# Second MoE in two phases per 768 tokens: gated values kept in SBUF, the output by seven block products, weights split once and streamed

## The chip, the cores and the metric

The kernel runs on one core of one Trainium2 chip. The metric is the device time of one execution in microseconds, as the median of several runs. A core has TensorE (matmuls, with a separate record for each weight load), VectorE, ScalarE, GpSimd and SyncE; here SyncE issues the DMAs. In the profile they are PE and PEld, DVE, ACT, POOL, and SP or SPq.

## What is computed

Three layers, one after the other, in float32:

```python
# attention, 4 x 8 heads x 768 positions x 64, chunks of 32 with a window of 56 and 8 memory keys
a = exp(scores - max); a = a / (sum(a) + 1e-09); out[chunk] = a @ v_full
x = out.transpose(0, 2, 1, 3).reshape(3072, 512)
# first MoE, d_ff = 2048
h = x @ w_in;  y = max(h, 0) ** 2 @ w_out
# second MoE, d_ff = 1536
g = y @ w_gate;  silu = g / (1 + exp(-g))
result = (silu * (y @ w_val)) @ w_out2          # 3072 x 512
```

Weights come as 64-bit floats and are turned into float32 on the chip. For precision each float32 operand is split into a high half (rounded to the matmul's type, float32r) and a low half (the rest), and each product is three passes: high x high, high x low, low x high.

## The kernel before

Attention for eight blocks of 384 tokens runs beside the first MoE. The first MoE works by block t and by f (16 blocks of 128 hidden columns): `hidden` (L413) issues 12 matmuls into one of two banks `hbank`, `relu`, `square`, `square_again` and `square_lo` make the halves of the squared values on ScalarE and VectorE, and `project` (L434) issues 12 matmuls into `ybank` two f later. In this part only TensorE's order is written by hand; the other engines' order comes from a planner that goes by its own costs and by due times. A due time is a count of quarter steps of f, `QB` = 64 of them per block.

In blocks 2 to 6 of the first MoE, 18 preps ready the second MoE's weights: `load2` (L455) fetches 1 MB into a tile `raw`, of which there are two, and `prep2` (L458) converts it (ScalarE, VectorE) to a tile `cut`. For two of three preps GpSimd makes four sums of 256 columns, and one to three DMAs store weights and sums, unsplit, to DRAM (`w2g`, `w2o`).

The second MoE takes 768 tokens at a time (s = 0 to 3), as two blocks of 384 tokens, and f = 0 to 11 (128 columns each of gate and value). Gate and value are computed together as a 2x2 block product by the Strassen-Winograd scheme: seven block products instead of eight (`gated`, L571), each of six matmuls of 384 columns, with the token sums T1 to T4 and the weight sums S1 to S4. VectorE combines the results; ScalarE applies Silu. Products alternate between the two banks `hbank`. Weights are loaded again for each f and each s, and split again (ScalarE the high half, GpSimd the low half: `split_w`, L481, through L92 and L95).

The output product follows at once: for each f, 18 matmuls of 512 columns (six groups of 128 tokens, three passes) add into six banks `outs` over all f (`output`, L617). `fill` (L762) puts them between the next f's products, six at a time. At f = 11 the banks are copied out and stored. In the second MoE the order on all engines is written by hand. `split_b1`, `sum_t` and `split_t` (L519 to L542) prepare the next 768 tokens during the current ones.

Of the kernel before, what the change touches and what calls it, by code (L numbers as in the profile page):

```python
# [19 lines left out]
GQ = 96  # L20
# [24 lines left out]
QC = 2 * 128  # L45
RAW = 2048
# [18 lines left out]
def attention_moe_moe_kernel(ctx, tc, att, v0, w1, w2, out):  # L65
# [132 lines left out]
    turned = [yb1[:, i, 0:NI * GQ].rearrange("p (j q) -> p j q", q=GQ) for i in range(2)]  # L198
# [253 lines left out]
    WAT = {n: i * QC for i, n in enumerate(("A11", "A12", "S2", "S3", "S1", "S4", "A22"))}  # L452
    w2t = {}
# [4 lines left out]
    def prep2(c):  # L458
        raw = w.pop(("raw2", c))
        a = convert(raw)  # L460
        if c % 3 == 2:
            sp.dma_start(out=w2o[c // 3], in_=a)
            return
        dst = w2g[c // 3 * 2 + c % 3]
        a11, a12, a21, a22 = (a[:, i * QC:(i + 1) * QC] for i in range(4))
        sums = raw.bitcast(F32)[:, 0:4 * QC]
        s2, s3, s1, s4 = (sums[:, i * QC:(i + 1) * QC] for i in range(4))
        for o, x, y, op in (
            (s1, a21, a22, ALU.add), (s2, s1, a11, ALU.subtract),
            (s3, a11, a21, ALU.subtract), (s4, a12, s2, ALU.subtract),  # L470
        ):
            pool.tensor_tensor(o, x, y, op)  # L472
        sp.dma_start(out=dst[:, 0:2 * QC], in_=a[:, 0:2 * QC])
        sp.dma_start(out=dst[:, 2 * QC:6 * QC], in_=sums)
        sp.dma_start(out=dst[:, 6 * QC:7 * QC], in_=a22)

    def fetch(key, raw, src, n):
        w["raw2", key] = raw[:, 0:n]
        sp.dma_start(out=raw[:, 0:n], in_=src)

    def split_w(key, part):  # L481
        raw = w["raw2", key]
        n = raw.shape[1] // 2
        if part == 0:
            w2t[key] = pair()
        c = slice(n * part, n * part + n)
        split(*(t[:, c] for t in w2t[key]), raw[:, c], act, pool)
# [3 lines left out]

    NGV = (4 * QC, 3 * QC)

    def load_gv(i, half):
        c = 4 * QC * half
        raw = rawp.tile([128, WC], F32, tag="cut", name="gvraw", bufs=CB)
        fetch((i, half), raw, w2g[seq2[i][1], :, c:c + NGV[half]], NGV[half])

    def split_gv(i, half, part):
        split_w((i, half), part)  # L500


    def load_out(i):
        fetch(("out", i), spare(), w2o[seq2[i][1] // 2], WC)

    def split_out(i, part):
        split_w(("out", i), part)
# [10 lines left out]

    def split_b1(s, k):  # L519
        if k == 0:  # L520
            zt[s] = {}
            zt[s]["x"] = [xp.tile([128, KD, NTM], R, tag=f"x{i}", name=f"z{i}") for i in range(2)]
# [4 lines left out]
    def sum_t(s, name):  # L527
# [3 lines left out]
        if name == "T2":  # L531
            t2 = spare()[:, 0:2 * NT2].rearrange("p (k n) -> p k n", k=2)
# [6 lines left out]
    def split_t(s, name):  # L539
        src = zt[s][name]  # L540
        zt[s][name] = [t[:, 0:2 * NT2].rearrange("p (k n) -> p k n", k=2) for t in pair()]
        split(*zt[s][name], src, act, dve)  # L542

    utile = {}

    def product(i, wname, zname, to):
        c = WAT[wname]
        whi, wlo = (t[:, c % WC:c % WC + QC] for t in w2t[i, c // WC])
        zh, zl = zt[seq2[i][0]][zname]
        n = 0  # L550
# [20 lines left out]
    def gated(i, fill, side):  # L571
# [29 lines left out]
        if not late:  # L601
            fill(6)
# [240 lines left out]
```

## Time and profile before

| | |
|---|---|
| median of the runs | 1170.83 us (1170.21 to 1172.29, 3 runs) |
| profiled execution, first to last instruction | 1170.6 us |
| TensorE busy | 1156.5 us, 8156 matmuls |
| VectorE, ScalarE, GpSimd busy | 673.3, 604.0, 354.2 us |
| DMA | 150.78 MB, mean 129 GB/s |

The span covers all work; the runs' median is 0.2 us above it. A listed duration of a matmul includes its way through the array, and matmuls overlap, so the time from one start to the next says what a matmul costs.

### The profile page before, as it was taken

The numbers are of one execution on the slowest core, as the hardware profiler recorded it, in microseconds if no ns is written. First come the engines' busy times: TensorE is split into PE (matmuls) and PEld (weight loads), VectorE is DVE, ScalarE is ACT, GpSimd is POOL, SyncE is SP. The second block draws the span as 40 slices with busy tenths as digits, with TensorE's granted clock in tenths as the row PEclk, the third lists the DMA queues.
The fourth block names the chain that finished last, engine by engine and source line by source line (L and its number), as shares of the span: only waits on it lengthen the run. The fifth ranks groups of instructions, "written<-read, shape, count | busy, mean of one in ns | idle before, by whom it ended". The sixth has DMA issues, their size and how long they took to land.

```text
span 1170.6 us, 20811 instructions
## 1 busy us (share of the span) xinstructions
PE 1156.5 (99%) x8156; PEld 1101.8 (94%) x8156; DVE 673.3 (58%) x1210; ACT 604.0 (52%) x1470; POOL 354.2 (30%) x299
## 2 busy tenths in 40 slices
PE   6999999999999999999999999999999999999998
PEld 5999999999999999999999999999999999999997
DVE  7897435547455474532415576656766576665554
ACT  5897445546455455554543444444445444553432
POOL 0000000203002021000034475555656465654551
PEclk9999999999999999999999999999999999999999
DMA  9732124527144272520124222353234433343231
GB/s 375 291 129 78 55 65 166 181 81 277 58 174 168 77 252 87 169 87 18 56 81 145 99 99 95 136 184 114 89 123 153 149 107 105 100 147 131 84 111 55
DMA packets 49443, 150.78 MB, mean 129 GB/s; under 512 B 4800, under 2 KB 14528, under 8 KB 44992
## 3 DMA queue, kind: packets, MB, share of 16 engines
q1 hardware_dynamic: 49344, 149.44, 36.8%
q8 instruction: 64, 1.05, 0.4%
q14 instruction: 35, 0.29, 0.1%
HBM read 122.68 MB, written 26.74 MB: 128 GB/s over the span
## 4 chain that ended last, share of the span: by engine, by line
PE 98%; DMA 1%; DVE 0%; SPq 0%; ACT 0%; issue 0%; DVEq 0%; ACTq 0%
PE hbank L553 30%; PE hbank L385 23%; PE yb L429 23%; PE yb L627 11%; PE abank L627 6%; PE abank L282 2%; PE abank L160 2%; PE hbank L220 1%; DMA first_v<-in_v_dram 1%; DMA out_dram<-o 0%; PE yb L202 0%; SPq L135 0%; DVE tmp L592 0%; DVE tmp L593 0%; DVE o L631 0%
## 5 line engine op out<-in xcount | busy, mean ns | idle before, releaser
L95 POOL TENSOR_TENSOR w<-gvraw,w 128x512 fp32r<-128x512 f32 x192 | 247.6, 1311 | 294.4 <-ACT w L92 294.4
L385 PE MATMUL hbank<-x,w 128*128 128x384 f32 (+1 forms) x1548 | 293.1, 338 | 0.0
L553 PE MATMUL hbank<-w 128*128 128x384 f32 x1440 | 281.8, 335 | 0.1
L385 PEld LDWEIGHTS hbank<-x,w 128*128 128x128 f32 x1548 | 272.9, 191 | 0.8 <-issue 0.2
L553 PEld LDWEIGHTS hbank<-w 128*128 128x128 f32 x1440 | 254.5, 188 | 9.2 <-DVE tmp L593 0.8
L429 PE MATMUL yb<-gh,w 128*128 128x384 f32 x1024 | 205.0, 337 | 0.0
L429 PEld LDWEIGHTS yb<-gh,w 128*128 128x128 f32 x1024 | 178.7, 188 | 2.2
L410 DVE TENSOR_TENSOR gl<-r,gh 128x384 fp32r<-128x384 f32 x128 | 74.2, 581 | 181.1 <-ACT r L404 180.6
L472 POOL TENSOR_TENSOR wraw<-cut 128x256 f32<-128x256 f32 x24 | 19.7, 842 | 445.7 <-DVE mx L228 285.7
L562 ACT CAST uh<-tmp 128x384 fp32r<-128x384 f32 x96 | 49.4, 514 | 185.1 <-DVE tmp L597 152.4
L393 ACT ACTIVATE r<-hbank 128x384 f32<-128x384 f32 x128 | 63.0, 492 | 146.9 <-PE hbank L385 146.9
L627 PE MATMUL yb<-w,uh 128*128 128x512 f32 x384 | 119.5, 392 | 0.0
L553 PE MATMUL hbank<-z,w 128*128 128x384 f32 x576 | 115.6, 335 | 0.0
L429 PE MATMUL yb<-gl,w 128*128 128x384 f32 x512 | 113.2, 334 | 0.0
L553 PEld LDWEIGHTS hbank<-z,w 128*128 128x128 f32 x576 | 102.1, 188 | 4.2
L92 ACT CAST w<-gvraw 128x512 fp32r<-128x512 f32 x192 | 99.2, 564 | 3.1 <-POOL w L95 2.1
L429 PEld LDWEIGHTS yb<-gl,w 128*128 128x128 f32 x512 | 90.9, 188 | 0.0
L236 ACT ACTIVATE prob<-abank,mx 96x72 f32<-96x72 f32 x224 | 68.2, 317 | 39.4 <-DVE mx L228 39.0
L263 DVE STREAM_TRANSPOSE pT<-prob 32x256 f32<-32x256 f32 x196 | 85.2, 435 | 3.2
L627 PEld LDWEIGHTS yb<-w,uh 128*128 128x128 f32 x384 | 70.7, 188 | 9.2
L627 PE MATMUL abank<-w,uh 128*128 128x512 f32 x192 | 74.9, 397 | 0.0
L399 ACT ACTIVATE gh<-r 128x384 fp32r<-128x384 f32 x128 | 67.4, 528 | 3.3
(97 smaller groups left out, 1278.8 us busy)
## 6 DMA issues: line engine op xcount, KB each, us to landing
wraw<-in_w_dram SPq DMA_DIRECT2D x34, 1024.0 KB, 8.1
gvraw<-w2g SPq DMA_DIRECT2D x48, 512.0 KB, 3.6
gvraw<-w2g SPq DMA_DIRECT2D x48, 384.0 KB, 3.1
qk<-in_att_dram SPq DMA_DIRECT2D x28, 464.0 KB, 3.9
spare<-w2o SPq DMA_DIRECT2D x24, 512.0 KB, 4.4
v<-in_att_dram SPq DMA_DIRECT2D x28, 256.0 KB, 3.5
y1d<-ys SPq DMA_DIRECT2D x8, 768.0 KB, 3.8
w2g<-wraw SPq DMA_DIRECT2D x12, 512.0 KB, 3.1
```

What stands on the lines that cost most here:

```text
L92: act.copy(hi, src)
L95: lo_engine.tensor_tensor(lo, src, hi.bitcast(F32), ALU.subtract)
L236: act.activation(probs[u % 2][:, h, 0:WK], s["s"][:, r, i], AF.Exp, bias=s["mx"][:, r, i:i + 1], scale=SCALE, accum_out=s["sm"][:, h],)
L263: dve.transpose(pT[row:row + 32, :, 32 * c:32 * c + 32], probs[u % 2][32 * c:32 * c + 32, :, col:col + 32],)
L385: pe.matmul(hbank[f % 2][:, cols], wt[:, k * 128:(k + 1) * 128], x[:, k, cols], start=i == 0, stop=i == 3 * KD - 1,)
L393: act.activation(r, hbank[f % 2][:, 0:n], AF.Relu)
L399: act.activation(gh, gtile[t, f]["r"], AF.Square)
L410: dve.tensor_tensor(gl, g["r"], g["gh"].bitcast(F32), ALU.subtract)
L429: pe.matmul(ybank[e][:, 0:nt_of[t]], wt[:, c:c + 128], gtile[t, f][g], start=f == 0 and p == 0, stop=f == NF1 - 1 and p == 2,)
L553: pe.matmul(to, wt[:, k * 128:k * 128 + 128], z[:, k], start=n == 0, stop=n == 5)
L562: act.copy(uh, u)
L627: pe.matmul(outs[j], u[:, c:c + 128], wt, start=f == 0 and p == 0, stop=f == NF2 - 1 and p == 2)
```

## The change

The second MoE keeps its scheme for gate and value, but works in two phases per 768 tokens. In the first phase all 84 gate and value products run one after the other, in four PSUM banks (`abanks`: the two `hbank` and two taken from `yb1`); the gated values u (six pairs of f, each with four blocks A11, A21, A12, A22) stay in SBUF in six tiles `uf`. GpSimd makes the sums S1 to S4 of the blocks of u.

In the second phase the output product is a Strassen-Winograd product too: seven block products (`ITEMS`), each over six pairs p, so 42 items. An item is nine matmuls of 256 columns: three groups of 128 tokens, three passes, with the halves of a block of u as weights and the output weights as moving data. Each block product fills 768 columns of PSUM (`pbank`, two of them in turn), and `combine` adds them up, on VectorE but for the first. The halves of u pass through a ring of ten pairs of tiles; the first ten splits are made in the first phase, each other one ten items ahead of its use. The next tokens are prepared in the second phase.

Weights and weight sums, those of the output weights too, are split in `prep2` and stored as 126 chunks of 256 KB (`w2d`), in the order of use. They are streamed four at a time into five tiles, once per 768 tokens; `load_chunks` for a group is called after the last product of the fifth group ahead of it. The due times of the preps move from (12, 26, 40, 52) to (4, 18, 32, 44) in each block.

The diff, cut to its core:

```diff
+NP = NF2 // 2
+GVC, WOC = 7 * NF2, 7 * NP
+NCH = GVC + WOC
+NRING = 10
...
-    w2g = dp.tile([NF2, 128, 7 * QC], F32, name="w2g")
-    w2o = dp.tile([NF2 // 2, 128, 2 * DM], F32, name="w2o")
+    w2d = dp.tile([128, NCH, 2, QC], F32, name="w2d")
     y1d = dp.tile([128, KD, NTOK], F32, name="y1d")
     hbank = [ps.tile([128, 512], F32, name=f"hbank{i}") for i in range(2)]
-    abank, yb0, yb1 = (ps.tile([128, 2, 512], F32, name=n) for n in ("abank", "yb0", "yb1"))
-    ybank = [b[:, i] for b in (yb0, yb1) for i in range(2)]
+    abank, yb0 = (ps.tile([128, 2, 512], F32, name=n) for n in ("abank", "yb0"))
+    yb1 = [ps.tile([128, 512], F32, name=f"yb1{i}") for i in range(2)]
+    ybank = [yb0[:, 0], yb0[:, 1], *yb1]
...
     def prep2(c):
         raw = w.pop(("raw2", c))
         a = convert(raw)
-        if c % 3 == 2:
-            sp.dma_start(out=w2o[c // 3], in_=a)
+        b0, b1, b2, b3 = (a[:, i * QC:(i + 1) * QC] for i in range(4))
+        sums = raw.bitcast(F32)[:, 0:4 * QC]
+        o0, o1, o2, o3 = (sums[:, i * QC:(i + 1) * QC] for i in range(4))
+        j, kind = divmod(c, 3)
+        if kind < 2:
+            jobs = ((o2, b3, b2, ALU.add), (o0, o2, b0, ALU.subtract), (o1, b0, b3, ALU.subtract), (o3, b1, o0, ALU.subtract))
+            first = 7 * (2 * j + kind)
+            places = [w2d[:, first:first + 3:2], w2d[:, first + 5:first + 6], w2d[:, first + 1:first + 4:2], w2d[:, first + 4:first + 7:2]]
+            parts = ((0, 2), (2, 4))
...
+        for o, x, y, op in jobs:
+            pool.tensor_tensor(o, x, y, op)
+        head = ap.tile([128, 2 * QC], R, tag="head", name="head")
+        pieces = [(a[:, 0:2 * QC], head), (b2, b3.bitcast(R))]
+        act.copy(head, a[:, 0:2 * QC])
+        pool.tensor_tensor(a[:, 0:2 * QC], a[:, 0:2 * QC], head.bitcast(F32), ALU.subtract)
+        act.copy(b3.bitcast(R), b2)
+        pool.tensor_tensor(b2, b2, b3, ALU.subtract)
+        hs = raw.bitcast(R)[:, 4 * QC:8 * QC]
+        act.copy(hs, sums)
+        pool.tensor_tensor(sums, sums, hs.bitcast(F32), ALU.subtract)
+        pieces += [(sums[:, m * QC:n * QC], hs[:, m * QC:n * QC]) for m, n in parts]
+        for place, (lo, hi) in zip(places, pieces):
+            for h, part in enumerate((hi.bitcast(F32), lo)):
+                sp.dma_start(out=place[:, :, h], in_=part.rearrange("p (n c) -> p n c", c=QC))
+
+    chunks = {}
+    NS = NTOK // (2 * NT2)
+
+    def load_chunks(g):
+        if 4 * g >= NS * NCH:
             return
...
+        t = chunks[g] = wp.tile([128, 4, 2, QC], R, tag="w", name="wst")
+        n = 0
+        while n < 4:
+            c = (4 * g + n) % NCH
+            m = min(4 - n, NCH - c)
+            sp.dma_start(out=t[:, n:n + m].bitcast(F32), in_=w2d[:, c:c + m])
+            n += m
...
+    uf, ring = [], []
+    SLOT = {"A11": 0, "A21": 1, "A12": 2, "A22": 3, "S3": 4, "S1": 1, "S2": 0, "S4": 2}
+    ITEMS = ("A11", "A12", "S2", "S3", "A22", "S1", "S4")
+    abanks = [*hbank, *yb1]
+    pbank = [b.rearrange("p a c -> p (a c)")[:, 0:2 * NT2] for b in (abank, yb0)]
...
+    def split_u(s, j, lo_engine):
+        i, p = divmod(j, NP)
+        hi, lo = ring[(WOC * s + j) % NRING]
+        split(hi, lo, u_of(p, ITEMS[i]), act, lo_engine)
...
+        if n % 4 == 3:
+            load_chunks(n // 4 + 5)
+
+    def gated(s, f, side):
+        n0 = NCH * s + 7 * f
+        b0 = 7 * (NF2 * s + f)
+        q = [abanks[(b0 + n) % 4][:, 0:NT2] for n in range(7)]
+        z = zt[s]
+        pair0, pair1, pair2 = double(), double(), double()
+        p1, u2 = pair0[:, 0:NT2], pair0[:, NT2:]
+        g0, u3 = pair1[:, 0:NT2], pair1[:, NT2:]
+        c22, u4 = pair2[:, 0:NT2], pair2[:, NT2:]
...
+    def item(s, j):
+        i, p = divmod(j, NP)
+        uh, ul = ring[(WOC * s + j) % NRING]
+        n = NCH * s + GVC + j
+        whi, wlo = chunk(n)
+        to = pbank[(7 * s + i) % 2]
+        for t in range(3):
+            rows = slice(128 * t, 128 * t + 128)
+            for m, (u, wt) in enumerate(((uh, whi), (ul, whi), (uh, wlo))):
+                pe.matmul(
+                    to[:, QC * t:QC * t + QC], u[:, rows], wt,
+                    start=p == 0 and m == 0 and t != 1, stop=p == NP - 1 and m == 2 and t != 0,
+                )
+        if n % 4 == 3:
+            load_chunks(n // 4 + 5)
...
+    def combine(s, i):
+        p = pbank[(7 * s + i) % 2]
+        if i == 0:
+            acc["x"] = double()
+            act.copy(acc["x"], p)
+        elif i == 2:
+            dve.tensor_tensor(acc["x"], p, acc["x"], ALU.add)
+        elif i == 3:
+            acc["y"] = double()
+            dve.tensor_tensor(acc["y"], p, acc["x"], ALU.add)
+        else:
...
     for c in range(NC2):
-        a = QB * (P2 + c // 4) + (12, 26, 40, 52)[c % 4]
+        a = QB * (P2 + c // 4) + (4, 18, 32, 44)[c % 4]
...
+    for s in range(NS):
+        for p in range(NP):
+            f = 2 * p + 1
+            job((s, f, 0), split_u, s, p, pool)
+            job((s, f, 1), sum_u, p, "S3")
+            last_pair = p == NP - 1
+            key = (s, "b", 0) if last_pair else (s, f + 1, 1)
+            job(key, sum_u, p, "S1")
+            job((s, "b", 0) if last_pair else (s, f + 1, 2), sum_u, p, "S2")
+            if NP + p < NRING:
+                job((s, f + 1, 4), split_u, s, NP + p, pool)
+            job((s, "b", 2 * NP + p), sum_u, p, "S4")
+        for j in range(NRING, WOC):
+            job((s, "b", j - NRING), split_u, s, j, pool if j % 3 == 2 else dve)
+        if s + 1 < NS:
+            job((s, 6, 3), load_z, s + 1)
+            for at_j, fn, *args in (
+                (0, split_b1, 0), (2, split_b1, 1), (4, sum_t, "T1"), (6, sum_t, "T3"), (8, sum_t, "T2"),
+                (10, sum_t, "T4"), (12, split_t, "T2"), (15, split_t, "T3"), (18, split_t, "T1"), (21, split_t, "T4"),
+                (24, split_t, "B22"),
             ):
-                job(i + at_f, slot, fn, s + 1, *args)
-    todo = iter(())
...
+    for s in range(NS):
+        for f in range(NF2):
+            gated(s, f, lambda slot: work(s, f, slot))
+        final = s == NS - 1
+        for j in range(WOC - NP * final):
+            item(s, j)
+            for args in ready:
+                store(*args)
+            ready.clear()
+            if j and j % NP == 0:
+                combine(s, j // NP - 1)
+            work(s, "b", j)
```

For the last 768 tokens the seventh block product runs as three rows of 18 matmuls (`item_rows`), and each row is added and stored by itself.

## Rows read from the trace of the kernel before

**Rows 1.** The page, part 1: busy us (share of the span), instructions, by engine.

```profile
PE 1156.5 (99%) x8156; PEld 1101.8 (94%) x8156; DVE 673.3 (58%) x1210; ACT 604.0 (52%) x1470; POOL 354.2 (30%) x299
```

**Rows 2.** The page, part 4: chain that ended last, by engine.

```profile
PE 98%; DMA 1%; DVE 0%; SPq 0%; ACT 0%; issue 0%; DVEq 0%; ACTq 0%
```

**Rows 3.** That chain in time, second MoE: start us, us, engine, target, line, count.

```profile
1092.01 3.14 PE hbank L553 x18
1095.15 0.47 PE yb L627 x2
...
1096.55 2.08 PE hbank L553 x12
...
1103.50 3.15 PE hbank L553 x18
```

**Rows 4.** Groups by form, second MoE: xcount | busy us, mean ns | idle before <-releaser.

```profile
L627 PE MATMUL yb<-w,uh 128*128 128x512 f32 x384 | 119.5, 392 | 0.0
L627 PE MATMUL abank<-w,ul 128*128 128x512 f32 x96 | 38.1, 397 | 0.0
L553 PEld LDWEIGHTS hbank<-w 128*128 128x128 f32 x1440 | 254.5, 188 | 9.2 <-DVE tmp L593 0.8
```

**Rows 5.** Timelines of TensorE in the opening: start us, us to the last end, what.

```profile
32.17 0.92 PE L385 MATMUL hbank<-x,w 128*128 128x288 f32 x3
32.89 0.49 PE L385 MATMUL hbank<-x,w 128*128 128x96 f32 x2
33.40 2.12 PE L385 MATMUL hbank<-x,w 128*128 128x96 f32 x9
35.32 0.97 PE L385 MATMUL hbank<-x,w 128*128 128x384 f32 x2
```

**Rows 6.** Timeline of weight loads after a stall near the end.

```profile
1159.60 0.30 PEld L553 LDWEIGHTS hbank<-w 128*128 128x128 f32 x2 [0.39 <-DVE tmp L593]
```

**Rows 7.** Groups by form, operations of the other engines that the change repeats or adds.

```profile
L578 DVE TENSOR_TENSOR tmp<-hbank,tmp 128x384 f32<-128x384 f32 x48 | 26.8, 557 | 43.6 <-ACT tmp L575 38.7 <-PE yb L627 3.0 <-PE hbank L553 1.1
L562 ACT CAST uh<-tmp 128x384 fp32r<-128x384 f32 x96 | 49.4, 514 | 185.1 <-DVE tmp L597 152.4 <-DVE tmp L609 31.1 <-PE hbank L553 1.0
L95 POOL TENSOR_TENSOR w<-gvraw,w 128x384 fp32r<-128x384 f32 x96 | 109.1, 1155 | 8.7 <-ACT w L92 8.7
L535 DVE TENSOR_TENSOR zraw<-zraw 128x768 f32<-128x768 f32 x8 | 10.9, 1364 | 3.0 <-DMA zraw<-y1d 3.0
L95 DVE TENSOR_TENSOR w<-zraw,w 128x768 fp32r<-128x768 f32 x16 | 17.7, 1106 | 7.8 <-ACT w L92 7.8
L372 ACT CAST w<-cut 128x1024 fp32r<-128x1024 f32 x16 | 16.8, 1049 | 0.9 <-DVE cut L368 0.9
L472 POOL TENSOR_TENSOR wraw<-cut 128x256 f32<-128x256 f32 x24 | 19.7, 842 | 445.7 <-DVE mx L228 285.7 <-DVE cut L113 119.3 <-DMA v<-in_att_dram 40.7
```

**Rows 8.** Timeline, first MoE, all engines (SPq is SP's DMA queue).

```profile
161.64 0.49 ACT L393 ACTIVATE r<-hbank 128x384 f32<-128x384 f32 x1 [2.46 <-PE hbank L385]
...
167.68 2.25 PE L385 MATMUL hbank<-x,w 128*128 128x384 f32 x12
...
205.21 1.53 POOL L472 TENSOR_TENSOR wraw<-cut 128x256 f32<-128x256 f32 x2 [8.76 <-DVE cut L113]
...
209.67 0.32 SPq L474 DMA_DIRECT2D w2g<-wraw  x1
...
210.51 0.78 SPq L141 DMA_DIRECT2D v<-in_att_dram  x1
```

**Rows 9.** Waits of ScalarE: line, waited for, us in total, times, longest us.

```profile
ACT wraw L110 <- DMA wraw<-in_w_dram: 35.0, 12, 6.2
```

**Rows 10.** Stretch 0 to 30 us: busy by engine, PEclk, DMA share, GB/s.

```profile
0.00:30.00 30.00, 20.21 (x406) 17.94 (x407) 20.86 (x40) 15.58 (x23) 1.75 (x10) 1.00 0.94 376
```

**Rows 11.** Timeline, the last matmul and the copy that follows it.

```profile
1166.01 0.39 PE L627 MATMUL abank<-w,ul 128*128 128x512 f32 x1
1166.76 0.69 DVE L631 COPY o<-abank 128x512 f32<-128x512 f32 x1 [0.94 <-DMA out_dram<-o]
```

More of the change, by code (lines that the diff above doesn't have):

```diff
@@ L489, in spare, with chunk @@
+    def chunk(n):
+        t = chunks[n // 4]
+        return [t[:, n % 4, h] for h in range(2)]
     def spare():
         return wp.tile([128, RAW], F32, tag="w", name="spare")[:, 0:WC]
[L492 to L504, printed above, removed]
@@ new lines, in gated @@
+    def gated(s, f, side):
[7 more added lines that the diff above has]
+        c22, u4 = pair2[:, 0:NT2], pair2[:, NT2:]
+        first, second = (u_of(f // 2, f"A{h}{f % 2 + 1}") for h in (1, 2))
+        product(n0, z["B11"], q[0])
+        act.copy(p1, q[0])
+        side(0)
+        product(n0 + 1, z["T2"], q[1])
+        dve.tensor_tensor(u2, q[1], p1, ALU.add)
@@ L594, in gated @@
         side(5)
-        product(i, "A22", "T4", q)
-        dve.tensor_tensor(u3, u3, q, ALU.subtract)
-        dve.tensor_tensor(u3, u3, g0, ALU.mult)
+        product(n0 + 6, z["B22"], q[6])
+        dve.tensor_tensor(u4, q[6], u4, ALU.add)
+        act.activation(u4, u4, AF.Silu)
+        dve.tensor_tensor(second, c22, u4, ALU.mult)
         side(6)
-        first = halves_of(u3)
-        late = i == len(seq2) - 1
-        if not late:
-            fill(6)
-        product(i, "S4", "B22", p)
@@ new lines, in item_rows, with store @@
+    def item_rows(s, t, to):
+        rows = slice(128 * t, 128 * t + 128)
+        for p in range(NP):
+            j = 6 * NP + p
+            uh, ul = ring[(WOC * s + j) % NRING]
+            whi, wlo = chunk(NCH * s + GVC + j)
+            for m, (u, wt) in enumerate(((uh, whi), (ul, whi), (uh, wlo))):
+                pe.matmul(to, u[:, rows], wt, start=p == 0 and m == 0, stop=p == NP - 1 and m == 2)
+    acc, ready = {}, []
+    def store(s, h, e, o, t0=0, n=3):
+        r0 = (2 * s + h) * NT2 + 128 * t0
+        sp.dma_start(
+            out=out[r0:r0 + 128 * n, e * QC:(e + 1) * QC].rearrange("(t p) c -> p t c", p=128),
+            in_=o.rearrange("p (t c) -> p t c", c=QC),
+        )
@@ L760, in attention_moe_moe_kernel, with job @@
[L760 to L775 removed]
+    def job(key, fn, *args):
+        jobs.setdefault(key, []).append((fn, args))
@@ new lines, in attention_moe_moe_kernel, with work @@
+    for _ in range(2):
+        t = rawp.tile([128, WC], R, tag="cut", name="ring", bufs=CB)
+        ring.append([t[:, 0:NT2], t[:, NT2:2 * NT2]])
+    def work(*key):
+        for fn, args in jobs.pop(key, []):
+            fn(*args)
+    for s in range(NS):
[10 more added lines that the diff above has]
+            work(s, "b", j)
+        if not final:
+            combine(s, 6)
+            for args in ready:
+                store(*args)
+            ready.clear()
```

219 lines of the change are left out of this document (80 added, 139 removed).

## Prediction

> **What bounds the kernel now.** I read the busy shares first: TensorE is busy 99% of the span, VectorE, ScalarE and GpSimd 58, 52 and 30% [rows 1]. A busy TensorE need not be full, so I read next what ended last: 98% of that chain is TensorE, following itself [rows 2]. In order of time the chain shows a steady beat inside the second MoE: 18 products, six output matmuls, 12 products and so on, again at the same place after 1103.50 - 1092.01 = 11.49 us [rows 3]. That is one f (a block of 128 gate and value columns); 48 of them are 551 us, nearly half the span. So the time is set by the columns that TensorE streams: an edit counts if it changes these, or makes TensorE wait where it doesn't now.
>
> The price of a matmul is its step from start to start; listed durations overlap. 18 matmuls of 384 columns take 3.14 us, 0.174 each; six of 512 lie between 1095.15 and 1096.55, 0.233 each [rows 3]: both 2.2 columns per ns, with no fixed part. An f is 42 of the one and 18 of the other; by columns 11.49 us splits into 42 x 0.1741 + 18 x 0.2321 = 7.31 + 4.18.
>
> **The change, part by part.**
>
> *Output product.* Before, 48 x 18 = 864 matmuls of 512 columns (four groups, 384 + 192 + 192 + 96, the first and the last in [rows 4]): 864 x 0.2321 = 200.5 us. After, per 768 tokens seven block products of six k-blocks, 9 matmuls of 256 columns each: 378, in all 1512. No row shows 256 columns with a full 128x128 weight. If columns alone count, a step is 0.1161 us, and all take 175.5 us: a gain of 25.0. The danger is the weight load, as every matmul brings new weights. The [rows 5] show where it bites. The opening ran at TensorE's lower level (1.2 GHz): three steps of 288 columns from 32.17 to 32.89, 0.240 each, 1.2 columns per ns. But nine steps of 96 columns, from 33.40 to 35.32, took 0.213 each and not 0.08. That floor is the load of 128 weight columns, and since 288 columns show nothing of it, a step is the larger of the two, not their sum. At the upper level (2.4 GHz), after a stall, two loads take 0.30 us [rows 6], one of them 0.19 [rows 4], so they start 0.11 apart: the floor halves with the clock. 256 columns at 0.116 stand just above it. I take 0.116, by the row of 288 columns, which is nearest: an eighth above its floor it cost nothing; here the margin is 5%. The ends are 0.11 (166 us, 9 us less) and 0.174 (the step of 384, 263 us, 88 us more).
>
> The Trainium skill (TensorE: Matmul & The Clock Gate, The mechanism) says that weight loads overlap running matmuls only when their row groups differ. All weights here fill the 128 rows, so by it a step would be 0.11 + 0.116 us, and the output products 342 us, 141 more than now. The trace speaks against it: a step of 0.174 leaves no room for 0.11 + 0.174.
>
> *Gate and value products.* The same 2016 matmuls, but with no output matmuls between them, and with four PSUM banks instead of two. Per f VectorE has nine operations of 0.56 (L578) [rows 7], 5.0 us, and one wait for a Silu of some 0.7, against 7.31 us of TensorE; ScalarE has three of about 0.5 and at most one high half of u. A bank is wanted again three products later, 3.1 us; its slowest reader (two adds on one bank) needs 1.1. Cost nothing; if this cover is gone, a gap appears ahead of a product in every f. Gain: the two places where two banks had no filler (TensorE's loads waited for L593, 0.8 us [rows 4], half of it at 1159.60 [rows 6]).
>
> *Splits of u.* In the output phase each item (9 matmuls, 1.04 us) wants one split: ScalarE 0.51, then VectorE 0.56 for two items of three, GpSimd 1.16 for the third [rows 7]. In the first 25 items VectorE also prepares the next tokens: four sums of up to 1.36, seven low halves of 1.11, three block sums that I put at 1.1 for 768 columns, and 17 low halves of u: 5.5 + 7.7 + 3.3 + 9.5 = 26.0 us, in 25 x 1.04 = 26.0 us. It will fall behind a little. Cover: the ring holds ten items (some 8 us of lag), and a block sum's bank is wanted again five items later (about 4 us of lag). I take nothing; with VectorE a quarter slower, a lag of 6.5 us would cost 2 us in each of three phases, 6 us. The weight splits that leave the second MoE were in no chain (GpSimd was 70% idle): no gain.
>
> *Stream of weights.* 126 chunks of 256 KB per 768 tokens, 132 MB in all: 1 MB per 4.17 us, 252 GB/s, with z and outputs about 270. In the first 30 us the queue moved 376 GB/s [rows 10] (the clock column of that row reads 1.00, though the steps of rows 5 just behind it are those of the lower level; I go by the steps). A load is asked for four groups (16.7 us) ahead; SP carries nothing else but two loads of z and the stores, each behind one VectorE sum. Cost nothing; without that cover each late group holds TensorE.
>
> *Preparing in the first MoE.* Eighteen preps now make all sums and all splits. Per prep GpSimd has four sums of 0.84 [rows 7] and three low halves (in proportion to columns 0.8, 1.7 and 3.4), ending some 9 us after the join; ScalarE has three copies (0.4, 0.6, 1.05 by L562 and L372 [rows 7]), 37 us in all; SP has 132 small stores instead of 42. ScalarE's copies wait for GpSimd's sums, and Relu and Square queue behind them. SP's stores wait for GpSimd, and loads of qk and v queue behind those: already before, a load of v left at 210.51 behind a store that had waited until 209.67 [rows 8]. Cover: the Relu at 161.64 had to end by 167.68, when its bank is written again [rows 8], so ScalarE may be held 5.5 us; a landing held it up to 6.2 us, of 35.0 in all [rows 9], and TensorE's chain shows none of it [rows 2]. A prep's hold is at most GpSimd's four sums (205.21 to 209.67, 4.5 us [rows 8]) plus 0.4 + 1.05, less the 0.6 that runs beside them: 5.3 us. I take 0.5 us for all; the ends are 0 and 1 us per prep, 18 us. Below nothing is out, as TensorE has no wait here to give back.
>
> *Tail.* Now 0.36 us pass from the last matmul's end (1166.40) to its copy, which takes 0.69 [rows 11]; storing takes the rest to 1170.6. After, half the columns and bytes: about 0.4 less.
>
> **Sum**, against the profiled span of 1170.6 us (the runs' median is 0.2 above it): -25.0 - 0.8 - 0.4 + 0.5 = -25.7, so 1144.9, and with the 0.2 around it **1145.1 us**. After this TensorE still bounds; VectorE in the output phase is next.
>
> **Rivals.** *The weight load sets the step,* by a hand-over that 288 columns had room to hide. At 0.128 us, 1512 x 0.012 = 18 more: 1163. For it: only 5% of margin; against it: a plain maximum in rows 5. Chance 0.09. *Shorter steps:* at 0.11 the products take 9 us less: 1136. Against it: 2.2 columns per ns at both widths of rows 3. Chance 0.05. The Trainium skill (same page, Back-to-back issue gap) has columns / 2.4 + 2.5 ns, 0.109 us here; for 384 columns that is 0.1625, where the trace has 0.174. *VectorE lags* in the output phase: 1151, chance 0.06. *Slower: ScalarE is held by GpSimd in the preps.* If ScalarE's written order expects the sums sooner than they end, each prep holds it past 5.5 us and the next hidden product waits. The time is worse than before from 25.7 / 18 = 1.4 us per prep; at 2 us it is 1145 + 36 = 1181. For it: GpSimd's four sums already take 4.5 us instead of 3.4 beside a busy VectorE; against it: even then the hold works out at 5.3. Chance 0.09 for this, 0.05 for a few us of it (1150 to 1160). *The stream is the bound:* 143 MB at 260 GB/s last 550 us, as long as the second MoE now; at 250, 572 us, 1192. Against it: 376 measured. Chance 0.04. *Columns don't fall,* since a product is left over: the diff's loops exclude it.
>
> **How the numbers follow.** Forecast 0.62, its own range 1142 to 1150. The range 1141 to 1163 leaves out the shorter steps below, the slow rivals and a part of the weight load above, 0.2 in all; the far end of 0.174 lies in that part. Faster by over 0.2% (2.3 us, about what a measurement tells from no change): forecast, shorter steps, lag, weight load up to 0.128 and the small prep stalls, 0.82 of 0.87, since some of these reach further; within 0.2%: 0.05; slower: 0.13.
>
> **What would show it.** Starts of 256-column matmuls 0.116 us apart; a chain of 84 products of 1.04 us, then 42 items of 1.04; no gap of TensorE at the preps; the DMA near 270 GB/s throughout. I would be wrong if items take 1.15 us or more (weight load), if gaps in the first MoE end with ScalarE (preps), if gaps end with a landing (stream), or with VectorE at every sixth item (lag).

## The result and the profile after

The changed kernel takes 1178.95 us (1178.58 to 1182.78), beside 1170.52 us (1169.68 to 1172.29) for the kernel before, measured with it: a ratio of 1.0079, interval 1.0061 to 1.0097. It is slower by 0.8%; 1145.1 us, in a range of 1141 to 1163, had been forecast.

The page, parts 1 and 4, answering [rows 1] and [rows 2]:

```profile
PE 1143.6 (97%) x8804; PEld 1126.0 (96%) x8804; DVE 725.8 (62%) x1216; ACT 545.0 (46%) x1348; POOL 338.8 (29%) x317
PE 58%; DVE 2%; ACT 0%; POOL 0%; issue 0%; ACTq 0%; DVEq 0%; POOLq 0%
```

TensorE's share of the chain fell from 98 to 58%: it begins only where some other engine last held TensorE up. The waits of TensorE (line, waited for, us in all, times, longest us) say which (`r` is the Relu's result, `ring` the high half of a block of u, `tmp` a block sum of `combine`):

```profile
PE hbank L389 <- ACT r L397: 18.3, 4, 4.6
...
PE abank L637 <- ACT ring L96: 2.3, 2, 1.2
...
PE yb L637 <- DVE tmp L668: 1.2, 1, 1.2
```

The first line is new and lies in the first MoE, whose matmuls the change didn't touch. How much is lost there shows in when the copies of `ys` at a block's end start. From the end of block 1 to that of block 5 (blocks are counted from 0, as in the code), before and after (timelines of ScalarE: start us, us, what):

```profile
185.65 1.05 ACT L444 COPY ys<-yb 128x384 f32<-128x384 f32 x2
479.09 1.05 ACT L444 COPY ys<-yb 128x384 f32<-128x384 f32 x2
```

```profile
182.41 0.84 ACT L448 COPY ys<-yb 128x384 f32<-128x384 f32 x2
503.87 0.84 ACT L448 COPY ys<-yb 128x384 f32<-128x384 f32 x2
```

293.4 us became 321.5: blocks 2 to 5, with 16 of the 18 preps, lost **28.0 us**. I use this difference below for each kernel ("loss in blocks 2 to 5"). It is that of the one profiled execution: the same first MoE lost 28.0, 27.5 and 28.4 (changed kernel, e3, e4) or 17.8 and 20.3 (e7, e10). It leaves out the opening, whose length varies without a cause that I traced: block 0's copies came between 108.5 and 112.4 us in all kernels but e11. From one start of a matmul to the next, 19.6 us of the loss are gaps (four of 4.75, two of 0.31); most of the rest is the clock. One gap and what follows (timeline of TensorE):

```profile
214.61 0.86 PE L433 MATMUL yb<-gl,w 128*128 128x384 f32 x4
220.06 3.73 PE L389 MATMUL hbank<-x,w 128*128 128x384 f32 x12 [4.59 <-ACT r L397]
...
225.89 2.24 PE L389 MATMUL hbank<-x,w 128*128 128x384 f32 x12
```

Twelve matmuls right behind the gap take 3.73 us instead of 2.24. The window from 220.00 to 223.40 (busy by engine, PEclk, DMA share, GB/s) has the granted clock at 0.59, mostly the lower level (1.2 GHz):

```profile
220.00:223.40 3.40, 3.35 (x12) 3.35 (x13) 1.80 (x5) 3.34 (x14) 1.57 (x1) 0.59 0.97 318
```

The second MoE did become shorter, from 551.8 to 535.1 us (first product to last matmul), as the chain of waits shows in time against [rows 3]:

```profile
726.85 6.47 PE abank L637 x54
733.32 6.48 PE yb L637 x54
739.80 6.48 PE abank L637 x54
746.28 6.49 PE yb L637 x54
753.88 6.70 PE abank L637 x54
```

54 matmuls of 256 columns (six items) take 6.48 us, 0.120 each. Between 752.77 and 753.88 there is a gap ahead of item 24, as in the next two phases. Two of the three are listed above as waits for ScalarE's `ring`, but that had ended at 753.37; what ended last, 0.1 us ahead of TensorE's start, was the block sum on VectorE, which reads the bank that item 24 writes (timeline):

```profile
752.84 0.94 DVE L668 TENSOR_TENSOR tmp<-abank,tmp 128x768 f32<-128x768 f32 x1
```

The profiled spans differ by 1177.5 - 1170.6 = 6.9 us: blocks 2 to 5 +28.0, the second MoE -16.7, the tail (last matmul to end) 4.2 to 3.0, so -1.2, and the opening -3.2 (block 1 ended at 182.41 instead of 185.65). From the end of block 5 to the second MoE both take 135.5 us. The medians differ by 8.4; the openings of two profiled executions need not be those of the others.

### The profile page after: what moved, and what is told of

Read it like the earlier page. It is cut to its first block, busy times and chain, and to the rows that moved or that the text cites. A ratio compares the mean times of both kernels' runs of the same rounds, so it can differ in the third digit from the quotient of the medians.

```text
span 1177.5 us, 22402 instructions
## 1 busy us (share of the span) xinstructions
PE 1143.6 (97%) x8804; PEld 1126.0 (96%) x8804; DVE 725.8 (62%) x1216; ACT 545.0 (46%) x1348; POOL 338.8 (29%) x317
## 3 DMA queue, kind: packets, MB, share of 16 engines
q8 instruction: 69, 1.13, 0.4%
## 4 chain that ended last, share of the span: by engine, by line
PE 58%; DVE 2%; ACT 0%; POOL 0%; issue 0%; ACTq 0%; DVEq 0%; POOLq 0%
PE hbank L586 15%; PE yb L586 15%; PE yb L433 7%; PE hbank L389 7%; PE abank L637 7%; PE yb L637 6%; DVE ring L99 1%; PE abank L286 0%; PE hbank L651 0%; DVE zraw L544 0%; DVE z L99 0%; PE abank L164 0%; DVE w L99 0%; POOL wraw L478 0%; PE yb L651 0%
## 5 line engine op out<-in xcount | busy, mean ns | idle before, releaser
L389 PEld LDWEIGHTS hbank<-x,w 128*128 128x128 f32 x1548 | 276.2, 193 | 20.4 <-ACT r L397 19.6
L414 DVE TENSOR_TENSOR gl<-r,gh 128x384 fp32r<-128x384 f32 x128 | 82.0, 642 | 201.9 <-ACT r L408 200.9
L99 POOL TENSOR_TENSOR ring<-uf,ring 128x384 fp32r<-128x384 f32 x84 | 97.4, 1162 | 273.8 <-PE hbank L586 141.7
L573 POOL TENSOR_TENSOR uf<-uf 128x384 f32<-128x384 f32 x96 | 109.5, 1156 | 124.0 <-DVE uf L625 124.0
L586 PE MATMUL yb<-w,wst 128*128 128x384 f32 x720 | 138.3, 334 | 0.0
L586 PE MATMUL hbank<-w,wst 128*128 128x384 f32 x720 | 138.3, 334 | 0.0
L397 ACT ACTIVATE r<-hbank 128x384 f32<-128x384 f32 x128 | 63.0, 492 | 147.7 <-PE hbank L389 144.3
L586 PEld LDWEIGHTS yb<-w,wst 128*128 128x128 f32 x720 | 126.0, 188 | 0.0
L586 PEld LDWEIGHTS hbank<-w,wst 128*128 128x128 f32 x720 | 126.0, 188 | 0.0
L96 ACT CAST ring<-uf 128x384 fp32r<-128x384 f32 x168 | 85.9, 511 | 58.2 <-PE yb L637 28.9
L637 PE MATMUL abank<-wst,ring 128*128 128x256 f32 x756 | 93.1, 283 | 2.3 <-ACT ring L96 2.3
L637 PEld LDWEIGHTS abank<-wst,ring 128*128 128x128 f32 x756 | 91.8, 192 | 2.6 <-ACT ring L96 2.6
L637 PE MATMUL yb<-wst,ring 128*128 128x256 f32 x702 | 86.4, 283 | 1.2 <-DVE tmp L668 1.2
L637 PEld LDWEIGHTS yb<-wst,ring 128*128 128x128 f32 x702 | 85.2, 192 | 1.4 <-ACT ring L96 1.4
```

Of the source, the lines that this page charges most:

```text
L96: act.copy(hi, src)
L99: lo_engine.tensor_tensor(lo, src, hi.bitcast(F32), ALU.subtract)
L389: pe.matmul(hbank[f % 2][:, cols], wt[:, k * 128:(k + 1) * 128], x[:, k, cols], start=i == 0, stop=i == 3 * KD - 1,)
L397: act.activation(r, hbank[f % 2][:, 0:n], AF.Relu)
L414: dve.tensor_tensor(gl, g["r"], g["gh"].bitcast(F32), ALU.subtract)
L573: pool.tensor_tensor(u_of(p, o), u_of(p, x), u_of(p, y), op)
```

## Experiments

**Where it happens.** Around the first gap ScalarE shows this (timeline):

```profile
211.11 0.46 ACT L297 CAST x<-abank 128x384 fp32r<-128x384 f32 x1
214.43 0.62 ACT L481 CAST head<-cut 128x512 fp32r<-128x512 f32 x1 [2.86 <-issue]
215.89 0.41 ACT L483 CAST cut<-cut 128x256 fp32r<-128x256 f32 x1 [0.84 <-POOL wraw L478]
217.37 1.04 ACT L486 CAST wraw<-wraw 128x1024 fp32r<-128x1024 f32 x1 [1.08 <-POOL wraw L478]
218.32 0.31 ACT L240 ACTIVATE prob<-abank,mx 96x72 f32<-96x72 f32 x1
...
219.51 0.49 ACT L397 ACTIVATE r<-hbank 128x384 f32<-128x384 f32 x1
```

From the end of L297 (211.57) to the Relu (L397, 219.51) 7.94 us pass: 2.86 of waiting for the prep's join (L117, VectorE's last step of the conversion, which ends at 214.36), 3.98 for its three copies with their waits, 1.10 for four exps of attention. TensorE would have gone on at 215.30, 3.7 us after ScalarE entered this stretch; 7.94 + 0.55 (the Relu and the hand-over) - 3.73 is the gap. VectorE and GpSimd show why the join was late (timelines):

```profile
209.61 2.40 POOL L487 TENSOR_TENSOR wraw<-wraw 128x1024 f32<-128x1024 f32 x1
```

```profile
210.21 2.22 DVE L414 TENSOR_TENSOR gl<-r,gh 128x384 fp32r<-128x384 f32 x1 [4.03 <-ACT r L408]
212.36 0.68 DVE L115 TENSOR_SCALAR wraw<-wraw 128x1024 int32<-128x1024 int32 x1
213.13 1.23 DVE L117 SCALAR_TENSOR_TENSOR cut<-wraw 128x1024 int32<-128x1024 int32 x1
```

`gl` (L414), otherwise 0.56, took 2.22 and ended just after GpSimd's low half of 1024 columns. The Trainium skill (SBUF — State Buffer, Who interferes with whom) says that VectorE and GpSimd share a pair of ports, that the first of them to start holds it for its whole instruction, and that a VectorE operation with two SBUF inputs contends with a GpSimd one that reads SBUF. The rows agree: 1.66 us more, beside the one operation. The prediction had weighed no such rule.

That ScalarE came to this stretch only 3.7 us ahead of TensorE's need has a like cause, one prep earlier (timelines of GpSimd, VectorE and ScalarE). The normalizing of attention (L258), 0.75 us in e15, took 2.90 beside a low half; the join behind it came late, and ScalarE waited 3.80 us for it.

```profile
195.71 2.41 POOL L487 TENSOR_TENSOR wraw<-wraw 128x1024 f32<-128x1024 f32 x1 [0.17 <-ACT wraw L486]
195.83 2.90 DVE L258 TENSOR_TENSOR prob<-prob,sm 96x576 f32<-96x576 f32 x1
204.28 0.62 ACT L481 CAST head<-cut 128x512 fp32r<-128x512 f32 x1 [3.80 <-DVE cut L117]
```

Both recur ahead of the other three gaps (`gl` 2.23 us, L258 2.90).

**First round.** Kernels without a ratio ran once. Theory A: ScalarE's copies, standing ahead of a Relu, hold TensorE. e1 moves the copies to GpSimd:

```diff
-        act.copy(head, a[:, 0:2 * QC])        # and b3, hs
+        pool.tensor_copy(head, a[:, 0:2 * QC])
```

> The kernel after, with the three copies of each prep (high halves) made by GpSimd instead of ScalarE; nothing else. Theory A (ScalarE, held by the prep's copies and by what the planner put behind them, makes Relu late): the four gaps of TensorE in the first MoE (4.7 us each, at 215, 295, 376 and 456 us of the profile after) and the stretches at the lower clock behind them vanish, the second MoE starts near 614 us instead of 639, and the time is near 1154 us. Theory B (the preps load GpSimd and its neighbour VectorE too much, the join comes late): GpSimd has 5 us more per prep, so the gaps stay or grow, and the second MoE starts at 639 us or later. Theory C (the moved due times are the cause): no change from the kernel after, 1179 us.

1183.06 us, ratio 1.009 (1.0068 to 1.0112), a loss of 33.5 us in blocks 2 to 5. Theory A, alone, fell: ScalarE is rid of the copies, yet its exps of attention wait 4.11 us for VectorE, behind the join, and the Relu behind them. This profile is of an execution 3.5 us above the median. Now the join itself stood beside GpSimd's low half (timelines of GpSimd and of VectorE):

```profile
212.08 2.82 POOL L487 TENSOR_TENSOR wraw<-wraw 128x1024 f32<-128x1024 f32 x1
```

```profile
213.13 2.85 DVE L117 SCALAR_TENSOR_TENSOR cut<-wraw 128x1024 int32<-128x1024 int32 x1 [0.49 <-DMA w2d<-cut]
```

e2 takes the due times back to `(12, 26, 40, 52)`:

> The kernel after, with the preps' due times set back to (12, 26, 40, 52). Theory C: the gaps in the first MoE vanish, about 1154 us. Theory A: the planner starts a prep as soon as a raw tile is free and its data are there, and puts the same operations ahead of Relu, so at least three of four gaps of 4.7 us stay, and the time is within 6 us of 1179.

1182.19 us, loss 27.3: the due times aren't the cause. The planner spaced the preps within a block nearly as in the changed kernel. e3 adds 400 matmuls behind the end, of several widths and with 128 or 64 weight columns:

```diff
...
+    for width, cols in ((128, 128), (192, 128), (224, 128), (256, 128), (288, 128), (320, 128), (384, 128), (256, 64), (384, 64), (256, 128)):
+        for n in range(40):
...
+            pe.matmul(..., start=True, stop=True)
```

> The kernel after, with 400 further matmuls at its end that nothing reads, ten forms of 40 each, every one with new weights: 128, 192, 224, 256, 288, 320 and 384 columns with weights of 128 columns, 256 and 384 columns with weights of 64 columns, and 256 with 128 again. Theory P (2.22 columns per ns, no fixed part, beside a floor from the weight load): 288 columns 0.130 us, 320 0.144, 384 0.173; 256 with 64 weight columns 0.116, and only 256 with 128 weight columns 0.120, held by the load. Theory F (a fixed part of 0.013 us beside 2.4 columns per ns): 288 columns 0.133, 320 0.147, 384 0.173, and 256 columns 0.120 with 64 and with 128 weight columns alike. By both, 128 columns stand at the load's floor, about 0.11.

| columns | 128 | 192 | 224 | 256 | 288 | 320 | 384 |
|---|---|---|---|---|---|---|---|
| us from start to start, 128 weight columns | 0.111 | 0.111 | 0.113 | 0.120 | 0.131 | 0.147 | 0.173 |
| the same, 64 weight columns | | | | 0.114 | | | 0.173 |

The floor of 0.111 is there, as the prediction had it, but near it the two bounds don't meet in a corner: 256 columns cost 0.120, and 0.114 with half the weight columns. So 0.006 of a matmul goes with the weight load, although that is the shorter of the two. Neither theory holds: P wanted 0.144 for 320 columns, F 0.120 for 256 with 64 weight columns too.

e4 spreads the preparation of the next tokens over items 0 to 35 instead of 0 to 24:

```diff
-                (0, split_b1, 0), (2, split_b1, 1), (4, sum_t, "T1"), ... (24, split_t, "B22"),
+                (0, split_b1, 0), (3, split_b1, 1), (6, sum_t, "T1"), ... (35, split_t, "B22"),
```

> The kernel after, with the next tokens' preparation spread over items 0 to 35 of the output phase instead of 0 to 24. Theory L (VectorE lags there and adds the block sum late): the three gaps of 1.3 us ahead of item 24, in the first three output phases, vanish; the second MoE is 4 us shorter (531 instead of 535), the first one unchanged with its gaps, so about 1175 us. Rival (GpSimd's low halves of u come late, or the ring is too short): the gaps stay, or move to other items, and the second MoE stays within 1 us of 535.

The second MoE is 531.0 us instead of 535.1, and no L637 is left among TensorE's waits: the three gaps were VectorE's lag, and cost 4.1 us. The whole stayed at 1178.62 (one run): it lost 28.4 in blocks 2 to 5, and its opening was 3.1 us longer than that of the changed kernel's profile.

**Second round: GpSimd's low halves.** e5 cuts the low halves of 512 and 1024 columns into pieces of 256, so that one operation holds the ports for less time. e6 has the pieces and the copies on GpSimd. e7 has the copies on GpSimd and the low halves on VectorE. e8 is e6 with the spreading of e4. The edit of the longest low half, with e7's line in place of the loop marked:

```diff
-        pool.tensor_tensor(sums, sums, hs.bitcast(F32), ALU.subtract)
+        for m in range(4):                                               # e5, e6, e8
+            x = slice(m * QC, m * QC + QC)
+            pool.tensor_tensor(sums[:, x], sums[:, x], hs[:, x].bitcast(F32), ALU.subtract)
+        dve.tensor_tensor(sums, sums, hs.bitcast(F32), ALU.subtract)     # e7
```

> The kernel after, with GpSimd's low halves of 512 and 1024 columns in each prep cut into operations of 256 columns; the high halves stay on ScalarE. In the profile after, VectorE's operation took 2.22 us instead of 0.56 while GpSimd's 1024-column subtraction ran (210.2 us), so the join came late, ScalarE waited 2.9 us for it, and Relu stood behind. Theory D (one GpSimd operation keeps VectorE out for its whole length): with pieces of 0.73 us VectorE is never kept out longer, the join comes 1.5 to 2 us earlier, and the four gaps of 4.7 us shrink to between 2 and 3.5; ScalarE's other waits stay. Theory A alone (ScalarE's copies and what the planner puts behind them): the gaps stay at 4.7.

> As the first experiment (high halves on GpSimd), with the low halves cut into operations of 256 columns. Theory D with A: with high halves on GpSimd and the long subtractions whole there were still about twenty gaps of 0.2 to 3.4 us in the first MoE, each behind a VectorE operation kept out by GpSimd; in pieces they fall to under a third of that, and the second MoE starts within 6 us of where the kernel before has it. Rival (GpSimd's total work keeps VectorE late, however it is cut): the gaps keep their sum, since the pieces add some 0.7 us of fixed cost per prep.

> High halves of the preps on GpSimd, low halves on VectorE: no GpSimd operation longer than about 1 us is left, and none of the three long ones that read two operands. VectorE gets 2.3 us more per prep, 42 us in all. Theory D: VectorE's operations are no longer kept out, so the gaps behind it shrink, though VectorE now waits in order for GpSimd's copies. Rival (VectorE and ScalarE are late because of the order the planner writes, not because of the port): gaps behind VectorE stay or grow.

> The sixth experiment together with the next tokens' preparation spread over items 0 to 35. Theory D with A and L: 4 us less than the sixth experiment, with no gap in the output phases: 1152 to 1160 us, faster than the kernel before. If the first MoE keeps gaps of 20 us, 1172 or more.

e5: 1173.8 us, loss 21.0; the four gaps shrank from 4.75 to 3.4 to 4.0. But at the first of them ScalarE is held almost as long as before, 7.74 us instead of 7.94 (2.14 of waiting, 4.49, 1.11); the gap is shorter because ScalarE came 4.9 us ahead of TensorE's need, with L258 at 1.20. The low half in four pieces took 4.60 us instead of 2.40, and VectorE's two steps to the join, 0.68 and 1.23 in the changed kernel, both ran beside it (timelines):

```profile
210.15 4.60 POOL L491 TENSOR_TENSOR wraw<-wraw 128x256 f32<-128x256 f32 x4
```

```profile
211.24 1.23 DVE L115 TENSOR_SCALAR wraw<-wraw 128x1024 int32<-128x1024 int32 x1
212.56 1.58 DVE L117 SCALAR_TENSOR_TENSOR cut<-wraw 128x1024 int32<-128x1024 int32 x1
```

So VectorE lost less: L258, `gl` and these two took 1.4 us longer than alone, instead of 3.8. But GpSimd's own low half got slower, its next sums began later, and the copies behind them took 0.5 us more. e6: 1179.88, loss 26.4, a miss: less than a third had been expected to stay. e7: 1168.36, loss 17.8. e8: 1172.86, ratio 1.0013 (0.9996 to 1.0031): with the copies on GpSimd, the pieces and the spreading together no difference from the kernel before.

**Third round: which part.** e9 leaves the splits out of the preps; sums and stores stay.

> The kernel after, with the splits left out of the preps: no high and no low halves are made (three copies of ScalarE, three subtractions of GpSimd each), and the unsplit weights and sums are stored in both places, so the output is not the reference's; all sums, stores and the whole second MoE stay. Theory (the loss in the first MoE comes from the splits alone): no gap of TensorE there, the second MoE starts at about 614 to 616 us, its length stays 535, and the time is about 1154 us. Rival (the further sums of the output weights, the 132 stores or the traffic take part): gaps remain, and the second MoE starts at 620 us or later.

1150.86 us, loss 0.0 (182.09 to 475.53, 293.4), no gap there, no lower clock. Everything that the first MoE lost comes from copies and low halves; the sums, which ScalarE no longer waits for, the 132 stores and their bytes cost nothing more than before.

e10 is e7 with the spreading, and e11 asks for the preps further apart, three per block from block 1 on:

```diff
-        a = QB * (P2 + c // 4) + (4, 18, 32, 44)[c % 4]
+        a = QB * (1 + c // 3) + (4, 24, 44)[c % 3]
```

> The seventh experiment (high halves on GpSimd, low halves on VectorE) with the next tokens' preparation spread over items 0 to 35. Theory: the two edits add, 4.1 us less than the seventh experiment, about 1164 us, a little faster than the kernel before. Rival (the gain of the seventh was chance of a single run): 1171 or more.

> The tenth experiment with three preps in each of blocks 1 to 6 instead of four in each of blocks 2 to 6 (due times 4, 24, 44). In the seventh experiment each block of four had three gaps of 1.2, 0.3 and 1.9 us, around its second prep, where VectorE's halves and the attention of one unit meet. If the gaps come from preps that follow each other too closely, they fall by half or more, and the time is 1157 to 1162 us. If each meeting of a prep with an attention unit costs the same, six blocks bring as much as five or more: 1164 or above.

e10: 1164.53 us, ratio 0.9939 (0.992 to 0.9959), faster than before, although blocks 2 to 5 still lose 20.3 in the profiled execution, which is 4.9 us above the median (the first MoE is that of e7, so one execution differs from another by 2.6 here). e11: 1178.92, 1.0055 (1.0036 to 1.0075): the gaps of a block come back unchanged in blocks 2 to 5 and nearly so in block 1 (3.7 and 3.4 us), with 0.2 in block 6. Block 0 ends at 118.5 instead of at most 112.4: the first prep's low halves now stand there ahead of a low half of the first MoE's weights, and TensorE has a gap of 5.1 us. The run doesn't test distance. The planner left the first three preps of a block as far apart as they were: in e10 the joins of block 2 start at 190.9, 204.7 and 214.0 us, in e11 at 201.9, 215.7 and 225.0. It shows that a block loses the same without its fourth prep.

e12 makes the splits a step of their own, due 12 quarter steps after the sums:

```diff
...
+        at(a + 12, split2, c)       # the copies, the low halves and the stores of prep2
```

> One edit to the changed kernel: each prep is cut in two; the sums stay at the due time, and the three copies, the three low halves and the stores follow as a step of their own, due 12 quarter steps (about two thirds of an f) later. Operations and data are the same. Theory H (the gaps come since ScalarE's written order has a copy that waits for the prep's own chain ahead of a Relu): with the sums long done, ScalarE's waits in L486 for GpSimd fall from 13.6 us to under 3, and the gaps of TensorE in the first MoE from 19.6 us to under 8; the time near 1163. Rival W (GpSimd's low halves beside VectorE's work for attention do it, wherever the copies stand): the gaps stay at 14 to 22 us in all and only move, and the time stays between 1172 and 1182.

1178.39 us, loss 27.6. This run settles nothing: the planner left ScalarE's order at the gap as it was, the copies between L297 and the exps (timeline of ScalarE; L485 is the former L481):

```profile
210.66 0.48 ACT L297 CAST x<-abank 128x384 fp32r<-128x384 f32 x1
214.00 0.62 ACT L485 CAST head<-cut 128x512 fp32r<-128x512 f32 x1 [2.86 <-issue]
```

e13 leaves out the low halves alone, e14 the copies alone:

> The changed kernel with the three low halves on GpSimd left out of every prep; ScalarE's copies stay, and the high halves are stored twice (so the output lacks the low parts of the second MoE's weights). Sums, stores, bytes and the second MoE's instructions are the same. Theory H (ScalarE's copies stand ahead of a Relu and wait for the prep's chain): most of the gaps stay, 12 us or more of 19.6. Theory G (GpSimd's low halves keep VectorE out, and the copies cost nothing by themselves): gaps under 4 us, the second MoE starts within 4 us of e9's 611. If only both together do it, each of e13 and e14 has under half of the 19.6.

> The changed kernel with ScalarE's three copies left out of every prep; GpSimd's three subtractions stay, each reading its own tile twice instead of the tile and its high half, and what they write is stored twice (so the second MoE's weights are not the reference's). Theory G: gaps stay at 10 us or more, with VectorE's operations lengthened beside GpSimd's as in the changed kernel (2.2 us for L414 beside the 1024-column low half). Theory H: gaps under 4 us, the second MoE starts within 4 us of 611, although VectorE is lengthened all the same.

Block ends of e13 and of e14 (timelines of ScalarE):

```profile
185.75 0.85 ACT L448 COPY ys<-yb 128x384 f32<-128x384 f32 x2
487.79 0.85 ACT L448 COPY ys<-yb 128x384 f32<-128x384 f32 x2
```

```profile
185.74 0.85 ACT L448 COPY ys<-yb 128x384 f32<-128x384 f32 x2
487.71 0.85 ACT L448 COPY ys<-yb 128x384 f32<-128x384 f32 x2
```

Neither 0, copies alone 8.6, low halves alone 8.5 (with gaps of 6.8 and 8.1 us), both 28.0. Neither theory H nor theory G holds alone; together they cost 11 us more than their sum, the third case that was written down for e13. In e13 the same Relu stands behind the same copies, but ScalarE waits 1.13 instead of 2.86 us for the join, and the gap there is 2.08. In e14 at most half of the gaps' time lies behind VectorE. The two longest, 2.24 and 1.76 us, lie behind ScalarE's first step on the next weights, which waited 8.78 and 8.40 us for their landing with a Relu behind it (timeline of ScalarE); the first of these loads had left behind stores that waited for GpSimd's last low half.

```profile
298.62 1.15 ACT L114 ACTIVATE wraw<-wraw 128x1024 f32<-128x1024 f32 x1 [8.78 <-DMA wraw<-in_w_dram]
```

e15 then keeps the copies on ScalarE and gives the low halves to VectorE, with the spreading of e4:

```diff
-        pool.tensor_tensor(sums, sums, hs.bitcast(F32), ALU.subtract)     # and a, b2
+        dve.tensor_tensor(sums, sums, hs.bitcast(F32), ALU.subtract)
```

> Copies stay on ScalarE, the three low halves of a prep go from GpSimd to VectorE; the next tokens' preparation is spread as in e4 (second MoE 531.0 us long). If it is GpSimd's low halves that make the copies dear: blocks 2 to 5 lose between e13's 8.7 and 14 us against the kernel before, and the time is 1152 to 1159, better than e10's 1164.5. If it is the length of the chain and the work that the splits give to VectorE and ScalarE, whoever does it: they lose 18 us or more, as in e10 (20.4), and the time is 1162 or more.

**1156.66 us, ratio 0.9872 (0.9844 to 0.99)**: the fastest version with the whole computation. Blocks 2 to 5 lose 8.7 (182.03 to 484.17), as the copies alone do. The same work as in the changed kernel, with another engine for three lines, costs 19 us less there (the spreading by itself, e4, left this loss at 28.4). The stretch that held TensorE (timelines of VectorE and of ScalarE):

```profile
208.27 0.56 DVE L414 TENSOR_TENSOR gl<-r,gh 128x384 fp32r<-128x384 f32 x1 [0.29 <-ACT r L408]
208.83 0.70 DVE L115 TENSOR_SCALAR wraw<-wraw 128x1024 int32<-128x1024 int32 x1
209.62 1.23 DVE L117 SCALAR_TENSOR_TENSOR cut<-wraw 128x1024 int32<-128x1024 int32 x1
```

```profile
210.88 0.62 ACT L481 CAST head<-cut 128x512 fp32r<-128x512 f32 x1 [1.24 <-DVE cut L117]
...
216.04 0.48 ACT L397 ACTIVATE r<-hbank 128x384 f32<-128x384 f32 x1
```

`gl` takes 0.56 again, ScalarE's stretch is 216.04 - 209.64 = 6.4 us, and it begins 5.3 us ahead of TensorE's need instead of 3.7, so the gap is 1.65. The first gap in four kernels, in us (the hold is waiting, copies and exps; the lead is the time from ScalarE's entering the stretch to where TensorE would have gone on; the gap is the hold less the lead plus the 0.5 of the Relu and the hand-over):

| | waits for join | copies | exps | hold | lead | gap |
|---|---|---|---|---|---|---|
| after | 2.86 | 3.98 | 1.10 | 7.94 | 3.73 | 4.75 |
| e5, low halves in pieces | 2.14 | 4.49 | 1.11 | 7.74 | 4.87 | 3.40 |
| e13, no low halves | 1.13 | 4.08 | 1.09 | 6.30 | 4.76 | 2.08 |
| e15, low halves on VectorE | 1.24 | 4.06 | 1.10 | 6.40 | 5.28 | 1.65 |

In a table of loss in blocks 2 to 5:

| | low halves on GpSimd | on VectorE |
|---|---|---|
| copies on GpSimd | 33.5 (e1) | 17.8 (e7) |
| copies on ScalarE | 28.0 (after) | 8.7 (e15) |

## Why the prediction was wrong

*The preps: the step that failed.* "A prep's hold is at most GpSimd's four sums plus 0.4 + 1.05, less the 0.6 that runs beside them: 5.3 us", against a cover of 5.5, was one step with three faults. The part that it worked out, from the join to the end of the last copy, was too dear if anything (3.98 us). But it began at the join, while ScalarE comes to the copy ahead of it and waits (2.86); it ended at the last copy, while exps of attention stood between that and the Relu (1.10); 7.94 in all. And the cover was that of a Relu where ScalarE arrived in time; here 3.7 us were left. The low halves entered only as work ending "some 9 us after the join" on an idle engine, with durations longer than the real ones (0.8, 1.7 and 3.4 us; 0.75, 1.29 and 2.40 measured). They were 19 us dearer there than on VectorE (e15): ahead of each gap two VectorE operations stood beside them, 1.7 and 2.1 us too long.

*The size.* I took 0.5 us for all preps, with 1 us per prep as the far end. 28.0 us are 1.6 for each of 18. The slower rival had half of the mechanism, ScalarE held in the preps with the Relu behind it; it laid this to GpSimd's sums, which by themselves cost nothing (e9). It gave 1.4 us per prep as the point from which the kernel is slower; with the 17.9 that the second MoE and the tail really gained, the point was 1.0. It decided, and deserved more than 0.09. What the ends left out also was that a stall is paid twice: of the 28.0, about 8 us are matmuls at the lower clock behind the gaps.

*The output products.* Columns fell as said; but 0.116 was mis-sized by 0.004: 0.120 measured, 1512 x 0.0039 = 5.9 us. "By the row of 288 columns" was the wrong neighbour: there the margin over the load was an eighth, and at the upper clock too 288 take only what their columns ask, 0.131 (e3). It could say nothing of a margin of 5%, where a step costs more than either bound.

*VectorE in the output phase.* The lag was seen and taken as nothing; it cost 4.1 (e4). The duration failed: 0.56 was taken for a low half of u on VectorE and 1.11 for one of z, and they took (groups by form of the changed kernel)

```profile
L99 DVE TENSOR_TENSOR ring<-uf,ring 128x384 fp32r<-128x384 f32 x84 | 70.6, 855 | 15.1 <-ACT ring L96 15.1
L99 DVE TENSOR_TENSOR w<-zraw,w 128x768 fp32r<-128x768 f32 x16 | 22.6, 1412 | 0.4 <-ACT w L96 0.3
```

with GpSimd at work beside them. The 0.56 itself was right, also for a split with both inputs in SBUF: in the kernel before all 96 of these took 0.55 (group by form),

```profile
L566 DVE TENSOR_TENSOR ul<-tmp,uh 128x384 fp32r<-128x384 f32 x96 | 52.6, 548 | 0.6 <-ACT uh L562 0.6
```

and 46 of them ran beside GpSimd, but none began behind it. In the changed kernel 47 of the 84 low halves of u run alone or begin first, and take 0.54 to 0.56; the other 37 begin while a GpSimd operation runs, and take up to 1.39. For z it is the same: 0.94 to 0.96, or 1.77 for the nine that begin behind. Before, six of 16 did so, at 1.35. Spread out (e4), the mean of z is 1.106 again. So the durations of before failed here because more of these operations begin behind one of GpSimd's.

*What was right.* With -25.0 and -0.8 for the products and banks, +5.9 and +4.1, and 0.0008 less for each of 2016 matmuls of 384 columns (0.1733 instead of 0.1741, -1.6), the second MoE should have gained 17.4; it gained 16.7. The phase of gate and value has no gap. The weight load doesn't add to the matmul: 0.120 is far from 0.11 + 0.116. The stream is no bound, with 5.0 us to landing and no wait:

```profile
wst<-w2d SPq DMA_DIRECT2D x124, 1024.0 KB, 5.0
```

The tail, put at 0.4, gained 1.2.

*What stays open.* Whether the copies, which alone cost 8.6, would cost less in another place: e12, meant for that, left ScalarE's order unchanged, and with a hold of 6.3 to 6.4 us against a lead of 4.8 to 5.3 (table) the first gap is there even without a low half on GpSimd. Why copies on GpSimd are dearer than on ScalarE (both columns of the last table) and why pieces helped so little there (e6) I didn't trace.

## What to carry to other kernels

Work given to an idle GpSimd isn't free when VectorE is in the path: look at each VectorE operation that begins behind a GpSimd one (here 0.56 us became 2.22), and take durations from a stretch where both are busy. To bound a hold on an in-order engine, count from when the engine reaches the waiting instruction to the one that the bottleneck needs, with whatever stands between, and set that against the slack at that very place. Near the floor of a weight load, a step is a little above the larger of the two times (here 0.120 us, beside 0.116 and 0.111).

## Not expected of the hardware

- After each of the four gaps of 4.75 us TensorE ran at the lower granted clock for 3.4 or 6.8 us. After the 2.08 us gap of e13 it did so for 3.4 us, after gaps of 1.3 us in the output phases not at all, and in e14 not after one of 2.24 us. The loss of a stall can be half as much again as the stall.
- VectorE's 384-column subtraction took 2.22 us instead of 0.56 beside one GpSimd operation of 2.40, and a join of 1.23 took 2.85 beside one of 2.82 (e1). The one that begins first decides: beside a GpSimd operation that began later, VectorE's low halves of u kept their 0.54 to 0.56. The same 1024-column subtraction takes 1.22 us on VectorE (mean of 18 in e15) and 2.40 on GpSimd.
- 256 columns take 0.120 us with 128 weight columns and 0.114 with 64, at one and the same clock.
